# A transform and two feed-forward layers in float32r: operand tiles of 512 columns in place of 502, and padded constants

## The chip, the core and the metric

The kernel runs on one NeuronCore of a Trainium2 chip. The metric is the device time of one execution in microseconds (us). TensorE (PE in the profile) multiplies: it first loads a block of weights (PEld, 128 rows by 128 columns) and then streams a second operand, the moving one, past it, one column after the other. VectorE (DVE), ScalarE (ACT) and GpSimd (POOL) do the elementwise work, and SyncE (SP) issues most transfers. All operands of TensorE lie in SBUF, the on-chip memory of 128 partitions; an address below is a byte offset within a partition.

## The reference

`x` is 2 x 3008 x 256. Its two-dimensional Fourier transform is taken and the real part kept; the 6016 rows of 256 go through two layers of one shape, 256 to 2048 to 256, with different nonlinearities.

```python
X = np.fft.fft(np.fft.fft(x, axis=1), axis=2).real      # 2 x 3008 x 256
x = X.reshape(6016, 256)
h = x @ w_in;   x = (h * sigmoid(h)) @ w_out             # layer 1
h = x @ w_in2;  y = (h * clip(h + 3, 0, 6) / 6) @ w_out2 # layer 2
```

## The kernel before, in words

The transform (the first 50 us or so) is done with float32 matmuls against tables: `step1` (47-point, table `t1_sb`), `step2` (256-point, `t2_sb`) and `step3` (64-point, `t3_sb`), lines 350 to 413. Each float32 matmul stands as two records in the trace. The result is kept as even and odd parts in the tile `eo`, which has 3010 columns.

The layers work on six chunks of those columns, five of 502 and one of 500 (`CHUNK` and `CHUNKS`, lines 52 and 53). Precision comes from splitting each operand into a rounded high part and a remainder, both float32r (4 bytes an element), and from three matmuls for each product. That is `mm3`, lines 299 to 302, through which all the layers' matmuls go:

```python
T.matmul(o, wh, xhi, ...)   # L300: high weights, high data
T.matmul(o, wh, xlo, ...)   # L301: high weights, low data
T.matmul(o, wl, xhi, ...)   # L302: low weights, high data
```

The second argument is the weights, the third the moving operand; each of the three loads its weights anew. There are 3888 such matmuls: 3240 of 502 columns and 648 of 500.

Layer 1 runs to about 435 us of the span. `win1` and `win1_end` (551 to 573) multiply the chunk's even part, then its odd part, into `ab`; the moving operands are the halves `[:, 0]` and `[:, 1]` of the tiles `xhi` and `xlo` from `split_eo` (504). ScalarE makes `ghi`, GpSimd and VectorE make `glo` (`low`, 616), both tiles of two halves as well, and `wout1` (630) multiplies their halves into four accumulators (`y` in the rows). Layer 2 computes the hidden products by seven products instead of eight (`pa`, `pb`, `pc`, `pd`; loop from 880 on): its moving operands are the tiles `b11` to `b22` and `t1` to `t4` (`b` and `t` in the rows), made by `moving` (668), and part of its weights are sums of blocks in the tile `wx` (`load_w2`, 262). `wout2` (814) uses `ghi` and `glo` as `wout1` does.

Where these tiles begin matters to the change, so here is what the built program gives. `ghi`, `glo`, `xhi` and `xlo`, and four of the ten ring buffers of `moving` (pool `xsp`), are tiles of 2 x 502 elements, 4016 bytes a partition. Each begins 32 bytes past a multiple of 64. Its half `[:, 0]` therefore starts at 32 past, and its half `[:, 1]`, 2008 bytes later, at 56 past. The other six ring buffers (pool `xq`) are 2 x 512, and both their halves start at a multiple of 64. All the layers' weights, in `whi`, `wlo` and `wx`, start at 32 past a multiple of 64: three single-column constants `three`, `mask` and `minus` of 4 bytes, each in a slot of 32, stand ahead of them in the memory. Counted over the 3888 matmuls, the moving operand starts at

| past a multiple of 64 | which operands | matmuls | of 502 / 500 columns |
|---|---|---|---|
| 32 bytes | halves `[:, 0]` | 1704 | 1416 / 288 |
| 56 bytes | halves `[:, 1]` | 1572 | 1308 / 264 |
| 0 | both halves of the six `xq` buffers | 612 | 516 / 96 |

The order of the work is written out by hand: the loops issue each engine's instructions in the order in which they stand, and semaphores release them.

Of the kernel before, what the change touches and what calls it, by code (L numbers as in the profile page):

```python
# [36 lines left out]
F32 = mybir.dt.float32  # L37
F32R = mybir.dt.float32r
U32 = mybir.dt.uint32
I32 = mybir.dt.int32  # L40
AF = mybir.ActivationFunctionType
# [3 lines left out]
S, D, B = 3008, 256, 2  # L45
# [4 lines left out]
FF, P = 2048, 128  # L50
NF = FF // P
CHUNK = 502
CHUNKS = [(c, min(CHUNK, NPAIR - c)) for c in range(0, NPAIR, CHUNK)]


# [11 lines left out]
NEAR = 4  # L67
# [13 lines left out]
def body(tc, xh, x128, t1, t2, t3, w1, w128, w2, out):  # L81
    nc = tc.nc
    V, A, T, G = nc.vector, nc.scalar, nc.tensor, nc.gpsimd
    per = tc.alloc_tile_pool(name="per", bufs=1)
# [3 lines left out]
    eop = tc.alloc_tile_pool(name="eop", bufs=1, side="right")  # L88

    w128_sb = per.tile([P, NF], F32, name="w128_sb")  # L90
    three = per.tile([P, 1], F32, name="three")
    mask = per.tile([P, 1], F32, name="mask")
    minus = per.tile([P, 1], F32, name="minus")
    eo = eop.tile([P, 2, NPAIR], F32, name="eo", tag="eo")
    w2_d = [
        [dr.tile([P, 2, n], F32, name=f"w2{q}_d{g}", tag=f"w2{q}_d{g}") for q, n in (("h", 512), ("l", 512), ("x", 384))]
# [110 lines left out]
    wx = []  # L207
# [53 lines left out]

    def load_w2(g):
        if not wx:
            wx.append(eop.tile([P, NF // 2, 2, 384], F32R, name="wx", tag="eo"))
        weight_tiles(2, g)
        for dst, src in zip((whi[2, g], wlo[2, g], wx[0][:, g]), w2_d[g]):
            nc.sync.dma_start(dst.bitcast(F32), src)
# [37 lines left out]
    fft = tc.alloc_tile_pool(name="fft", bufs=1)  # L305
# [3 lines left out]
    nil = fft.tile([P, P], F32, name="nil")  # L309
    w128_raw = fft.tile([P, NF, 2], U32, name="w128_raw")  # L310
    t1_sb = fft.tile([P, 6 * 104], F32, name="t1_sb")
    t2_sb = fft.tile([P, 257], F32, name="t2_sb")
    sign = t2_sb[:, 256:257]
    t3_sb = fft.tile([P, P], F32, name="t3_sb")
    xl = fft.tile([P, 2, B, 2, 32], F32, name="xl")
    xr = fft.tile([P, B, 12], F32, name="xr")
    out1 = [fft.tile([P, 2, QA, 2, NJ], F32, name=f"out1_{n}") for n in range(B)]
    xt = {}
    xbuf = [xp.tile([P, k, 4 * P], F32, name=f"x{i}", tag=f"x{i}") for i, k in enumerate((1, 2, *[XB] * 4))]
# [51 lines left out]
    def step1_last():  # L371

        ps = psA.tile([P, 512], F32, name="psl", tag="s2")
        for n in range(B):
            for j in range(4):
                T.matmul(
                    ps[32 * j : 32 * j + 32, 12 * n : 12 * n + 12], xl[:, 0, n, j % 2, :],
                    t1_sb[:, 576 + 12 * j : 588 + 12 * j], start=True, stop=True,
                )
        A.activation(xr.rearrange("p n q -> p (n q)"), ps[:, 0:24], AF.Copy)  # L380


    def step2(g):
# [47 lines left out]
    A.dma_start(t1_sb[:, 0:288], t1[:, 0:288])  # L431
    for i in range(4):
        load_x(i, nc.sync, A)
    warm = fft.tile([P, 1], F32, name="warm")
    A.activation(warm, three, AF.Silu)
    V.memset(mask, 1.0)
    V.memset(mask[0:1], 0.0)
# [9 lines left out]
    i = g = 0  # L447
    busy(8)

    def step1_next():  # L450

        nonlocal folded, i
        x = folded
        if i + 1 < nx:
            folded = fold(i + 1)
        step1(i, x)
        if 3 <= i < nx - 4:
            load_x(i + 4, nc.sync, nc.sync)
        if i + 4 == nx - 1:
            load_raw(1, w1, 0)  # L460
        i += 1
        if i == 1:
            nc.sync.dma_start(t2_sb, t2)
            nc.sync.dma_start(t3_sb, t3)
            nc.sync.dma_start(xl, x128)
        if i < 3:
            busy(3 - i)
        if i == 4:
            nc.sync.dma_start(w128_raw, w128)
        if i == 5:  # L470
            G.tensor_tensor(out=xl[:, 0], in0=xl[:, 0], in1=xl[:, 1], op=ALU.add)
        if i == 7:
            step1_last()
        if i == nx - 4:
            load_raw(1, w1, 1)
            advance(steps, 1)
# [10 lines left out]
    while XCH[i][0] == 0:  # L487
        step1_next()
# [12 lines left out]
    xsp = tc.alloc_tile_pool(name="xsp", bufs=1, side="right", reuse_waits="tile")  # L501
    xs = {}

    def split_eo(k, j):
        c, n = CHUNKS[j]
        hi, lo = (xsp.tile([P, 2, CHUNK], F32R, name=f"x{h}{k}", tag=f"x{2 * (k % 2) + i}") for i, h in enumerate(("hi", "lo")))
        eb = xsp.tile([P, CHUNK], F32, name=f"eb{k}", tag="eb", bufs=2)
        new = k < len(CHUNKS)
        if new:
            nc.sync.dma_start(e128_d[j], eo[0:1, 1, c : c + n])  # L510
        nc.sync.dma_start(eb[:, :n], e128_d[j].to_broadcast([P, n]))
        if new:
            split(hi[:, :, :n], lo[:, :, :n], eo[:, :, c : c + n], x_d[j])
        else:
            for x, d in zip((hi, lo), x_d[j]):
                nc.sync.dma_start(x[:, :, :n].bitcast(F32), d)
        return hi, lo, eb
# [3 lines left out]
    units = [(k, f) for k, (_, fs) in enumerate(segs) for f in fs]  # L521
    n1 = NF * len(CHUNKS)
    turn = n1 - 10
# [4 lines left out]
    gs = {}  # L528

    def hidden_tiles():  # L530
        h = pools[0].tile([P, 2, CHUNK], F32, name="h", tag="h", bufs=2)
        ghi = pools[0].tile([P, 2, CHUNK], F32R, name="ghi", tag="ghi", bufs=4)
        return h, ghi

    def product(o, wt, x, first=True):
# [2 lines left out]
    begun, spare = {}, {}  # L538

    def even_part(k, f):  # L540

        i = units.index((k, f))
        if i < 4:
            if i % 2 == 0:
                spare[0] = pools[0].tile([P, 2, CHUNK], F32R, name=f"zg{i}", tag="glo").bitcast(F32)
            return spare[0][:, i % 2]
        if i == 4:
            spare[0] = stage_tile(1).rearrange("p m (s n) -> p (m s) n", s=2)
        return spare[0][:, i % 4]
# [25 lines left out]
    def parts(k, f):  # L575
# [6 lines left out]
    pools = [  # L582
        tc.alloc_tile_pool(name="wk", bufs=3, side="right", reuse_waits="tile"),
        tc.alloc_tile_pool(name="psH", bufs=4, space=PSUM, side="right", reuse_waits="tile"),
    ]
# [25 lines left out]
    stp = tc.alloc_tile_pool(name="stp", bufs=1, reuse_waits="tile")  # L611
    xq = tc.alloc_tile_pool(name="xq", bufs=1, reuse_waits="tile")
# [3 lines left out]
    def low(k, f, shared=False):  # L616
        n = CHUNKS[segs[k][0]][1]
        h, ghi, _ = gs[k, f]
        glo = pools[0].tile([P, 2, CHUNK], F32R, name="glo", tag="glo")
        for s, eng in ((1, G), (0, V if shared or f % 2 else G)):  # L620
            eng.tensor_tensor(out=glo[:, s, :n], in0=h[:, s, :n], in1=ghi[:, s, :n], op=ALU.subtract)  # L621
        gs[k, f] = ghi, glo
# [45 lines left out]
    def moving(k):  # L668

        j = segs2[k][0]
        n = CHUNKS[j][1]
        st = stp.tile([P, 2, 2 * CHUNK], F32, name=f"u{k}", tag="su", bufs=1)
        nc.sync.dma_start(st[:, :, : 2 * n], y1_d[j])
        b11, b12 = st[:, 0, 0:n], st[:, 0, n : 2 * n]
        b21, b22 = st[:, 1, 0:n], st[:, 1, n : 2 * n]
        us[k] = {}

        def high(name, src):  # L680
            r = ring[0] % RING
            ring[0] += 1
            x = (xsp if r < NEAR else xq).tile([P, 2, CHUNK if r < NEAR else 512], F32R, name=f"{name}_{k}", tag=f"x{r}")
            us[k][name] = x[:, 0, :n], x[:, 1, :n]
            A.activation(x[:, 0, :n], src, AF.Copy)

        def rest(name, src):
            hi, lo = us[k][name]
            (V if k == 0 and name in ("b21", "t2", "t3") else G).tensor_tensor(out=lo, in0=src, in1=hi, op=ALU.subtract)

        yield
        high("b11", b11)
        yield
        rest("b11", b11)
        high("b21", b21)
        yield
        rest("b21", b21)
        yield
        V.tensor_tensor(out=b11, in0=b12, in1=b11, op=ALU.subtract)
        V.tensor_tensor(out=b12, in0=b22, in1=b12, op=ALU.subtract)  # L700
        high("t1", b11)
        yield
        rest("t1", b11)
        yield
        V.tensor_tensor(out=b11, in0=b22, in1=b11, op=ALU.subtract)
        V.tensor_tensor(out=b21, in0=b11, in1=b21, op=ALU.subtract)
        high("t2", b11)
        yield
        rest("t2", b11)
        high("t4", b21)  # L710
        yield
        rest("t4", b21)
        high("t3", b12)
        yield
        rest("t3", b12)
        high("b22", b22)
        yield
        rest("b22", b22)
        yield
# [25 lines left out]
    for i in range(n1):  # L745
        k, f = units[i]
# [26 lines left out]
        else:  # L773
# [4 lines left out]
            q, odd = divmod(i - turn, 2)  # L778
# [25 lines left out]
        E.tensor_tensor(out=g[1][:, i, :n], in0=h[:, i, :n], in1=g[0][:, i, :n], op=ALU.subtract)  # L804

    def split_tiles():
        h = pools[0].tile([P, 2, CHUNK], F32, name="h", tag="h", bufs=2)
        ghi = pools[0].tile([P, 2, CHUNK], F32R, name="ghi", tag="ghi", bufs=4)
        glo = pools[0].tile([P, 2, CHUNK], F32R, name="glo", tag="glo")
        return h, (ghi, glo)  # L810

    y2, kept2, late = {}, {}, []
# [45 lines left out]
            nc.sync.dma_start(out[:, m, c : c + n], dst)  # L858

    def snapshot(name, n):  # L860
        t = xsp.tile([P, CHUNK], F32, name=name, tag="eb", bufs=2)
        A.activation(t[:, :n], pa[:, :n], AF.Copy)  # L862
        return t

# [8 lines left out]
    for e, (k, f) in enumerate(units2):  # L873
        j, fs = segs2[k]
        n = CHUNKS[j][1]
        u = us[k]
# [210 lines left out]
```

## Time and profile before

| | |
|---|---|
| time, median of 3 runs | 942.62 us (942.47 to 942.95) |
| time of the profiled execution | 942.65 us |
| its span, first to last instruction | 940.9 us |
| TensorE busy | 935.5 us, 99% |
| weight loads busy | 778.5 us, 83% |
| VectorE / ScalarE / GpSimd busy | 70% / 69% / 56% |
| granted TensorE clock | 1.00 of full speed |

A matmul's own duration in the trace overlaps the next one's and its end is modelled, so the 390 ns of one is not what it costs. What it costs is read from the starts: the time from one matmul's start to the next one's, called the pitch below. The starts stand in the timeline, to 0.01 us, and the count of matmuls in a long stretch gives their mean. Weight loads have rows of their own on PEld.

### The profile page before, as it was taken

Reading aid. Unit: us, or ns where it says so; the run is one execution under the profiler, and the core shown is the slowest. Engines: PE = TensorE matmul, PEld = TensorE weight load, DVE = VectorE, ACT = ScalarE, POOL = GpSimd, SP = SyncE. Lnnn points to the kernel's source line nnn. Section 1 sums busy time; section 2 is a strip of 40 time slices with the busy share of each in tenths; the row PEclk is TensorE's granted clock in tenths of the full one; section 3 lists DMA queues with packets and bytes.
Section 4 is the critical chain, followed back from the end, with each engine's and each line's share of the span. In section 5 each row is a group of like instructions: output and inputs, shape, how many; then the busy total and the mean of one; then the engine's idle time right before and its main releaser. Section 6 shows DMA issues by size and latency. Waiting matters only on the chain.

```text
span 940.9 us, 12163 instructions
## 1 busy us (share of the span) xinstructions
PE 935.5 (99%) x4286; PEld 778.5 (83%) x4286; DVE 662.8 (70%) x907; ACT 651.5 (69%) x1144; POOL 531.0 (56%) x391
## 2 busy tenths in 40 slices
PE   9999999999999999999999999999999999999998
PEld 9988888888888888888888888888888888888886
DVE  7988899979999999865554565564555555455544
ACT  4878767675767676857776777766776677677665
POOL 2056646654666656534774567655765665476543
PEclk9999999999999999999999999999999999999999
DMA  8554344052263636576130002020020002001001
GB/s 320 193 203 149 134 143 144 1 189 97 104 217 121 191 119 192 189 279 211 62 88 1 1 1 88 0 88 1 1 88 0 1 1 88 1 0 44 1 1 44
DMA packets 25160, 89.27 MB, mean 95 GB/s; under 512 B 2886, under 2 KB 11340, under 8 KB 22572
## 3 DMA queue, kind: packets, MB, share of 16 engines
q1 hardware_dynamic: 23724, 81.81, 23.9%
q0 software_dynamic: 992, 6.16, 3.4%
q8 instruction: 33, 0.54, 0.2%
q10 hardware_dynamic: 384, 0.54, 0.2%
q14 instruction: 27, 0.22, 0.1%
HBM read 52.30 MB, written 36.20 MB: 94 GB/s over the span
## 4 chain that ended last, share of the span: by engine, by line
PE 99%; DMA 0%; ACT 0%; DVE 0%; issue 0%
PE y L300 19%; PE y L302 19%; PE y L301 19%; PE ab L300 5%; PE ab L301 5%; PE ab L302 5%; PE pa L301 4%; PE pa L300 4%; PE pa L302 3%; PE pb L301 2%; PE pb L302 2%; PE pb L300 2%; PE ps L365 1%; PE ps L408 1%; PE pd L301 1%; PE pc L301 1%
## 5 line engine op out<-in xcount | busy, mean ns | idle before, releaser
L804 POOL TENSOR_TENSOR glo<-h,ghi 128x502 fp32r<-128x502 f32 (+1 forms) x191 | 247.9, 1310 | 198.7 <-ACT ghi L801 198.7
L621 POOL TENSOR_TENSOR glo<-h,ghi 128x502 fp32r<-128x502 f32 (+1 forms) x137 | 218.3, 1609 | 193.3 <-ACT h L580 180.4
L300 PE MATMUL y<-ghi,whi 128*128 128x502 f32 (+1 forms) x768 | 299.6, 390 | 0.0
L302 PE MATMUL y<-ghi,wlo 128*128 128x502 f32 (+1 forms) x768 | 299.4, 390 | 0.0
L301 PE MATMUL y<-glo,whi 128*128 128x502 f32 (+1 forms) x768 | 299.4, 390 | 0.0
L301 PEld LDWEIGHTS y<-glo,whi 128*128 128x128 f32 x768 | 145.1, 189 | 30.4
L300 PEld LDWEIGHTS y<-ghi,whi 128*128 128x128 f32 x768 | 144.8, 189 | 30.7
L302 PEld LDWEIGHTS y<-ghi,wlo 128*128 128x128 f32 x768 | 144.5, 188 | 30.1
L801 ACT ACTIVATE ghi<-h 128x502 fp32r<-128x502 f32 (+1 forms) x192 | 118.0, 624 | 46.7 <-DVE h L796 46.7
L579 ACT ACTIVATE ghi<-ab 128x502 fp32r<-128x502 f32 (+1 forms) x96 | 56.5, 588 | 89.8 <-DVE h L570 88.6
L796 DVE SCALAR_TENSOR_TENSOR h<-h,pc 128x502 f32<-128x502 f32 (+1 forms) x96 | 65.1, 678 | 72.2 <-ACT h L793 72.2
L926 DVE TENSOR_TENSOR pc<-u,pb 128x502 f32<-128x502 f32 (+1 forms) x48 | 32.9, 685 | 114.6 <-ACT u L862 114.6
L862 ACT ACTIVATE u<-pa 128x502 f32<-128x502 f32 (+1 forms) x96 | 56.8, 591 | 59.1 <-PE pa L302 58.7
L793 ACT ACTIVATE h<-pc,three 128x502 f32<-128x502 f32 (+1 forms) x96 | 64.7, 674 | 40.4 <-DVE pc L926 37.7
L559 DVE SCALAR_TENSOR_TENSOR st<-eb,w_sb,ab 128x502 f32<-128x502 f32 (+1 forms) x92 | 67.0, 728 | 17.8 <-PE ab L302 17.6
L300 PE MATMUL ab<-xhi,whi 128*128 128x502 f32 (+1 forms) x192 | 75.4, 393 | 0.0
L301 PE MATMUL ab<-xlo,whi 128*128 128x502 f32 (+1 forms) x192 | 75.1, 391 | 0.0
L302 PE MATMUL ab<-xhi,wlo 128*128 128x502 f32 (+1 forms) x192 | 75.0, 391 | 0.0
L570 DVE SCALAR_TENSOR_TENSOR h<-st,ab 128x502 f32<-128x502 f32 (+1 forms) x92 | 61.4, 667 | 7.7 <-PE ab L302 7.1
L796 DVE SCALAR_TENSOR_TENSOR h<-h,pd 128x502 f32<-128x502 f32 (+1 forms) x96 | 64.4, 671 | 1.2 <-ACT h L793 1.2
L793 ACT ACTIVATE h<-pd,three 128x502 f32<-128x502 f32 (+1 forms) x96 | 64.8, 675 | 0.6 <-DVE pd L938 0.6
L580 ACT ACTIVATE h<-h 128x502 f32<-128x502 f32 (+1 forms) x96 | 60.0, 625 | 3.0
(167 smaller groups left out, 1580.8 us busy)
## 6 DMA issues: line engine op xcount, KB each, us to landing
raw<-in_w SPq DMA_DIRECT2D x16, 1024.0 KB, 7.0
u<-y_d SPq DMA_DIRECT2D x6, 1004.0 KB, 6.9
y_d<-st SPq DMA_DIRECT2D x5, 1004.0 KB, 4.3
y_d<-st POOLq DMA_DIRECT2D x5, 1004.0 KB, 8.4
out<-st SPq DMA_DIRECT2D x20, 251.0 KB, 2.2
w2h_d<-h SPq DMA_DIRECT2D x8, 512.0 KB, 2.6
w2l_d<-t SPq DMA_DIRECT2D x8, 512.0 KB, 2.6
whi<-w2h_d SPq DMA_DIRECT2D x8, 512.0 KB, 8.6
```

Of the source, the lines that this page charges most:

```text
L300: T.matmul(o, wh, xhi, start=first, stop=False, **group)
L301: T.matmul(o, wh, xlo, start=False, stop=False, **group)
L302: T.matmul(o, wl, xhi, start=False, stop=last, **group)
L559: V.scalar_tensor_tensor(out=z[:, :n], in0=eb[:, :n], scalar=w128_sb[:, f : f + 1], in1=ab[:, :n], op0=ALU.mult, op1=ALU.add)
L570: V.scalar_tensor_tensor(out=h[:, 0, :n], in0=z[:, :n], scalar=2.0, in1=ab[:, :n], op0=ALU.mult, op1=ALU.subtract)
L580: A.activation(h[:, s, :n], src, AF.Silu)
L621: eng.tensor_tensor(out=glo[:, s, :n], in0=h[:, s, :n], in1=ghi[:, s, :n], op=ALU.subtract)
L793: A.activation(h[:, i, :n], c[:, :n], AF.Relu, bias=three)
L796: V.scalar_tensor_tensor(out=h[:, i, :n], in0=h[:, i, :n], scalar=6.0, in1=c[:, :n], op0=ALU.min, op1=ALU.mult)
L801: A.activation(g[0][:, i, :n], h[:, i, :n], AF.Copy)
L804: E.tensor_tensor(out=g[1][:, i, :n], in0=h[:, i, :n], in1=g[0][:, i, :n], op=ALU.subtract)
L862: A.activation(t[:, :n], pa[:, :n], AF.Copy)
```

## The change

Every tile of 2 x 502 or 502 elements that holds a moving operand, or that shares memory with one, becomes 2 x 512 or 512 wide (`LINE = 512`); the same 502 or 500 columns are used. The constants `three`, `mask`, `minus` and `warm` become columns of one tile of 16 elements (64 bytes). `t2_sb`, `xr`, `wx` and the staging tile `u` are padded, so that what stands behind them starts at a multiple of 64 bytes.

In the built program all 3888 moving operands and all 3888 weight blocks of the layers start at a multiple of 64. Counted from a multiple of 128, the moving operands start at 64, the blocks in `whi` and `wlo` at 0, and those in `wx` at 64. In the transform most operands become aligned too.

No instruction is added, removed or moved: each of the five engines has the same rows in the same order. Three things differ in form. The copies of `xhi` and `xlo` run over 2 x 502 elements in place of 1004 that lie in one piece, on ScalarE and VectorE and in the transfers. The copy to `xr` writes 2 x 12 in place of 24. And around the start of layer 1, where the tiles take over the transform's memory, one copy of `xhi` and one transfer to `eb` no longer wait for what used that memory before, and a wait for two transfers passes from one copy of `ghi` to the next but one.

```diff
 CHUNK = 502
+LINE = 512
...
-    three = per.tile([P, 1], F32, name="three")
-    mask = per.tile([P, 1], F32, name="mask")
-    minus = per.tile([P, 1], F32, name="minus")
+    consts = per.tile([P, 16], F32, name="consts")
+    three, mask, minus, warm = (consts[:, i : i + 1] for i in range(4))
...
-            wx.append(eop.tile([P, NF // 2, 2, 384], F32R, name="wx", tag="eo"))
+            flat = eop.tile([P, NF * 384 + 8], F32R, name="wx", tag="eo")[:, : NF * 384]
+            wx.append(flat.rearrange("p (g i c) -> p g i c", i=2, c=384))
...
-    t2_sb = fft.tile([P, 257], F32, name="t2_sb")
+    t2_sb = fft.tile([P, 272], F32, name="t2_sb")
...
-    xr = fft.tile([P, B, 12], F32, name="xr")
+    xr = fft.tile([P, B, 16], F32, name="xr")
...
     def split_eo(k, j):
-        hi, lo = (xsp.tile([P, 2, CHUNK], F32R, name=f"x{h}{k}", tag=f"x{2 * (k % 2) + i}") for i, h in enumerate(("hi", "lo")))
-        eb = xsp.tile([P, CHUNK], F32, name=f"eb{k}", tag="eb", bufs=2)
+        hi, lo = (xsp.tile([P, 2, LINE], F32R, name=f"x{h}{k}", tag=f"x{2 * (k % 2) + i}") for i, h in enumerate(("hi", "lo")))
+        eb = xsp.tile([P, LINE], F32, name=f"eb{k}", tag="eb", bufs=2)
...
     def hidden_tiles():
-        h = pools[0].tile([P, 2, CHUNK], F32, name="h", tag="h", bufs=2)
-        ghi = pools[0].tile([P, 2, CHUNK], F32R, name="ghi", tag="ghi", bufs=4)
+        h = pools[0].tile([P, 2, LINE], F32, name="h", tag="h", bufs=2)
+        ghi = pools[0].tile([P, 2, LINE], F32R, name="ghi", tag="ghi", bufs=4)
...
-        glo = pools[0].tile([P, 2, CHUNK], F32R, name="glo", tag="glo")
+        glo = pools[0].tile([P, 2, LINE], F32R, name="glo", tag="glo")
...
     def moving(k):
-        st = stp.tile([P, 2, 2 * CHUNK], F32, name=f"u{k}", tag="su", bufs=1)
+        st = stp.tile([P, 4 * CHUNK + 8], F32, name=f"u{k}", tag="su", bufs=1)
+        st = st[:, : 4 * CHUNK].rearrange("p (m c) -> p m c", m=2)
...
-            x = (xsp if r < NEAR else xq).tile([P, 2, CHUNK if r < NEAR else 512], F32R, name=f"{name}_{k}", tag=f"x{r}")
+            x = (xsp if r < NEAR else xq).tile([P, 2, LINE], F32R, name=f"{name}_{k}", tag=f"x{r}")
```

The same replacement of `CHUNK` by `LINE` is made in `even_part`, `split_tiles` and `snapshot`.

## Rows read from the trace of the kernel before

**Rows 1.** The page: engines' busy time, granted clock, the chain that ended last.
```profile
PE 935.5 (99%) x4286; PEld 778.5 (83%) x4286; DVE 662.8 (70%) x907; ACT 651.5 (69%) x1144; POOL 531.0 (56%) x391
...
PEclk9999999999999999999999999999999999999999
...
PE 99%; DMA 0%; ACT 0%; DVE 0%; issue 0%
```

**Rows 2.** Waits of PE: who was waited for, us in total, times, longest.
```profile
PE psw L348 <- POOL nil L426: 1.0, 1, 1.0
PE ps L362 <- ACT out L367: 0.3, 1, 0.3
```

**Rows 3.** Windows, layers: busy us and instruction count by engine, clock, DMA share, GB/s.
```profile
60.00:936.00 876.00, 876.00 (x3837) 722.78 (x3837) 610.76 (x821) 609.10 (x1050) 516.12 (x376) 1.00 0.25 84
```

**Rows 4.** Timeline of PE, transform's end: start, us, engine, line, operation, operands.
```profile
43.95 0.47 PE L300 MATMUL ab<-xhi,whi 128*128 128x502 f32 x1
44.26 0.39 PE L301 MATMUL ab<-xlo,whi 128*128 128x502 f32 x1
...
46.42 0.47 PE L300 MATMUL ab<-xhi,whi 128*128 128x502 f32 x1
```

**Rows 5.** Timeline of PE, the aligned class's first, and the layers' last rows.
```profile
435.05 0.39 PE L300 MATMUL pa<-b,whi 128*128 128x502 f32 x1
...
923.69 0.39 PE L302 MATMUL pa<-t,wx 128*128 128x500 f32 x1
...
933.93 0.39 PE L302 MATMUL y<-ghi,wlo 128*128 128x500 f32 x1
...
936.41 0.39 PE L301 MATMUL y<-glo,whi 128*128 128x500 f32 x1
936.64 0.39 PE L302 MATMUL y<-ghi,wlo 128*128 128x500 f32 x1
```

**Rows 6.** Timeline of PEld in the transform; the last number counts the loads merged.
```profile
21.15 1.87 PEld L365 LDWEIGHTS ps<-t_sb,x 128*128 128x128 f32 x16
...
23.83 0.97 PEld L408 LDWEIGHTS ps<-t_sb,o 128*128 128x128 f32 x8
```

**Rows 7.** Timeline of PE in layer 2, products with `wx`.
```profile
604.31 0.39 PE L301 MATMUL pb<-t,wx 128*128 128x502 f32 x1
604.53 0.42 PE L302 MATMUL pb<-t,wx 128*128 128x502 f32 x1
604.78 0.41 PE L300 MATMUL pa<-t,wx 128*128 128x502 f32 x1
605.03 0.42 PE L301 MATMUL pa<-t,wx 128*128 128x502 f32 x1
605.28 0.40 PE L302 MATMUL pa<-t,wx 128*128 128x502 f32 x1
605.52 0.39 PE L300 MATMUL y<-ghi,whi 128*128 128x502 f32 x1
```

**Rows 8.** Timeline of PEld, the loads beside the first of these matmuls.
```profile
604.31 0.19 PEld L302 LDWEIGHTS pb<-t,wx 128*128 128x128 f32 x1
604.54 0.19 PEld L300 LDWEIGHTS pa<-t,wx 128*128 128x128 f32 x1
```

**Rows 9.** The transfers of `xhi` and `xlo`: count, KB each, median us to landing.
```profile
xh_d<-xhi SPq DMA_DIRECT2D x5, 502.0 KB, 4.6
...
xlo<-xl_d SPq DMA_DIRECT2D x5, 502.0 KB, 10.6
```

More of the change, by code (lines that the diff above doesn't have):

```diff
@@ L379, in step1_last @@
                 )
-        A.activation(xr.rearrange("p n q -> p (n q)"), ps[:, 0:24], AF.Copy)
+        A.activation(xr[:, :, 0:12], ps[:, 0:24].rearrange("p (n q) -> p n q", n=B), AF.Copy)
     def step2(g):
@@ L433, in body @@
         load_x(i, nc.sync, A)
-    warm = fft.tile([P, 1], F32, name="warm")
     A.activation(warm, three, AF.Silu)
@@ L462, in step1_next @@
         if i == 1:
-            nc.sync.dma_start(t2_sb, t2)
+            nc.sync.dma_start(t2_sb[:, 0:257], t2)
             nc.sync.dma_start(t3_sb, t3)
@@ L544, in even_part @@
             if i % 2 == 0:
-                spare[0] = pools[0].tile([P, 2, CHUNK], F32R, name=f"zg{i}", tag="glo").bitcast(F32)
+                spare[0] = pools[0].tile([P, 2, LINE], F32R, name=f"zg{i}", tag="glo").bitcast(F32)
             return spare[0][:, i % 2]
@@ L806, in split_tiles @@
     def split_tiles():
-        h = pools[0].tile([P, 2, CHUNK], F32, name="h", tag="h", bufs=2)
-        ghi = pools[0].tile([P, 2, CHUNK], F32R, name="ghi", tag="ghi", bufs=4)
-        glo = pools[0].tile([P, 2, CHUNK], F32R, name="glo", tag="glo")
+        h = pools[0].tile([P, 2, LINE], F32, name="h", tag="h", bufs=2)
+        ghi = pools[0].tile([P, 2, LINE], F32R, name="ghi", tag="ghi", bufs=4)
+        glo = pools[0].tile([P, 2, LINE], F32R, name="glo", tag="glo")
         return h, (ghi, glo)
@@ L860, in snapshot @@
     def snapshot(name, n):
-        t = xsp.tile([P, CHUNK], F32, name=name, tag="eb", bufs=2)
+        t = xsp.tile([P, LINE], F32, name=name, tag="eb", bufs=2)
         A.activation(t[:, :n], pa[:, :n], AF.Copy)
```

## Prediction

> **What bounds the kernel now.** I read the page first, then the waits of TensorE, then the timeline of TensorE and of its weight loads. On the page [rows 1] TensorE is busy for 935.5 of 940.9 us at a granted clock of 1.00, and the chain that ended last is 99% TensorE. In the list of its waits [rows 2] all of the span comes to 1.3 us. So no other engine and no transfer sets the time, and the only question is what one matmul costs.
>
> That isn't its duration but the pitch, from one start to the next. Between 60 and 936 us there are 3837 matmuls [rows 3], so 876 / 3837 = 228.3 ns each. The clock of 1.00 is the 2.4 GHz level, at which 502 columns, one a cycle, take 209.2 ns. Every matmul of the layers thus pays some 19 ns beyond its columns. I call that the excess; over all 3888 it is about 75 us, and only there can the place of operands matter.
>
> To see whether it matters I took the pitches from the timeline, subtracted the columns at 2.4 GHz, and averaged by where the moving operand starts past a multiple of 64 bytes. Ten pitches above 270 ns, around waits, and the last matmul are left out.
>
> - 32 past: 1699 pitches, the first starting at 43.95 us [rows 4], the last at 936.41 [rows 5]; excess 18.3 ns.
> - 56 past: 1568 pitches, from 46.42 [rows 4] to 933.93 [rows 5]; excess 19.7 ns.
> - 0 past: 610 pitches, from 435.05 to 923.69 [rows 5]; excess 20.8 ns. With weights in `whi` and `wlo` it is 18.9 (334 pitches), with `wx` 23.1 (276).
>
> The uncertainty of each of these means is 0.1 to 0.4 ns. The mean of all is 19.3 ns.
>
> So the aligned operands that the kernel already has are the dearest class, not the cheapest. But all weights stand at 32 past. What the cheapest class shares is that data and weights have the same place within 64 bytes.
>
> **The change part by part.**
>
> *Moving operands and weights.* The weights of the next matmul load while the present one streams: the loads start together with the matmuls, 604.31 and 604.31, 604.54 and 604.53 [rows 7, 8]. Two streams are read from the same memory at once, so I take the excess to depend on the place of one against the other. After the change the difference is 0 within 64 bytes for all pairs, as it is now for the 32-past class. Then the other two classes come down to 18.3 ns:
>
> - 1572 x (19.7 - 18.3) = 2.2 us,
> - 612 x (20.8 - 18.3) = 1.5 us,
>
> 3.7 us in all. No row shows weights at 0 past with a stream of 502 columns, so both ends have to be bounded. Downwards: the whole excess goes, 3888 x 19.3 = 75 us. Upwards: all pairs behave as the aligned data with `wx` do, 3888 x (23.1 - 19.3) = 15 us more. I take 3.7, from the nearest rows, those with the same difference.
>
> *The dear pairs.* In rows 7 the pitches from 604.53 on are 0.25, 0.25, 0.25 and 0.24 us. Of the 610 aligned pitches 54 are 240 to 250 ns, always with `wx`, and most come in such runs. Against 228 they cost 54 x 18 = 1.0 us, part of the 1.5 above. Most aligned pairs with `wx` run without it, so this is a state that a run of equal matmuls falls into. Data at 0 and weights at 32 past are gone after the change, but all pairs are then equal, which is the ground of a rival below.
>
> *The transform.* Its pitch is that of the weight loads: with `x` as weights (32 past), (1.87 - 0.19) / 15 = 112.0 ns; with `o` as weights and `t3_sb` as data, both already at a multiple of 64, (0.97 - 0.19) / 7 = 111.4 ns [rows 6]. These agree within the 0.01 us of the rows. I take 0 for some 400 records; a half nanosecond each would be 0.2 us.
>
> *Copies and transfers in other shapes.* The six copies each of `xhi` and `xlo` over 2 x 502 and the changed waits lie on engines that TensorE waits for by 1.3 us in the whole run [rows 2]; that is also the most that shifted waits can give back. The 24 transfers of `xhi` and `xlo` have rows of 2008 bytes where 4016 lay together. They land after 4.6 to 10.6 us [rows 9]. A loaded chunk is asked for at least five units ahead of its first use, and a unit is 18 matmuls, 4.1 us, so there are some 20 us of cover. If the landing doubled to 21.2 us, the six loads would come some 1 us late each, 6 us at most. I take 0, since the bytes are the same.
>
> *Elementwise work at aligned addresses.* GpSimd is busy 516 of 876 us and VectorE 611 [rows 3]. If they became a tenth slower or faster, TensorE would see it only through the waits of rows 2, so 0; the time from the last matmul at 936.64 us [rows 5] to the end of the span is a few copies and a transfer, and no term changes it.
>
> **Sum.** The profiled execution took 942.65 us, 0.03 above the median of 942.62, with 1.75 us outside its span. 942.65 - 3.7 = 938.9 us, 0.4% less.
>
> **A rule weighed.** The pitch of rows 3 is 228.3 ns. By the Trainium skill, "TensorE: Matmul & The Clock Gate", section "Back-to-back issue gap", an isolated warm matmul costs its columns at 2.4 GHz and 2.5 ns, measured on bf16; that is 211.7 ns here. The trace disagrees by 16.6 ns. If float32r at bad places were the whole cause, aligning would give 65 us, an estimate from that page. The third rival carries its chance, by the rows alone.
>
> **The rivals.**
>
> 1. *The place doesn't matter, only what runs beside it.* The means by class differ also in role: the 32-past ones are the first halves, the 0-past ones belong to layer 2 only. Then the aligned class keeps its present costs and all matmuls join it: 3456 with `whi` and `wlo` at 18.9 and 432 with `wx` at 23.1, together 75.3 us against 75.0 now. The time would be 943.0. For it: with `whi` the aligned class is within 0.6 ns of the best. Against it: halves 32 and 56 past alternate within the same unit, on the same engines' work, and still differ by 1.4 ns, many times the uncertainty.
>
> 2. *Slower: equal pairs lock into the dear state.* Now three kinds of places alternate, which breaks a run of equal matmuls after three to six. After the change every pair has the same places within 64 bytes, nothing breaks the run, and pitches of 0.25 us as in rows 7 become common. It decides from about 280 locked pitches more than now: at 18 to 20 ns each they outweigh the 3.7 us and 1.9 us beyond. If all went as the aligned class does on average, it is 3888 x (20.8 - 19.3) = 5.8 us more, 948.5; if as that with `wx`, 957.4. For it: the state occurs only where both data halves are aligned. Against it: it occurs only with data and weights 32 bytes apart, never in the 32-past class.
>
> 3. *A large gain.* If the excess is the price of weights at 32 past, it goes as a whole or in good part: 867 us at the most, 905 for half. For it: the excess is paid by all 3888 matmuls, and misplaced weights are the one thing that all share. Against it: the transform's loads have the same pitch with weights at 0 and at 32 past [rows 6], and data at 0 past gain nothing.
>
> 4. *Only the 56-past operands gain.* They alone start in the middle of 16 bytes; 0 and 32 are multiples. Then 1572 x 1.4 = 2.2 us goes and the rest stays: 940.4. The 0-past class at 20.8 against 18.3 speaks against it, its part with `whi` at 18.9 for it. This is the granularity that the Trainium skill gives in "SBUF — State Buffer", specifications: lines of 16 bytes. By that rule padding from 32 to 64 buys nothing; the trace neither confirms nor refutes it.
>
> **How the numbers follow.** Within 0.2%, about 1.9 us, a measurement of this kernel can't tell a difference from none. Chances: the forecast 0.35, with its own range 936 to 941; rival 1 0.25; rival 2 0.20; rival 3 0.10; rival 4 0.10. Faster: nearly all of the forecast (0.31), all of rival 3, more than half of rival 4 (0.06), 0.47. Within 0.2%: the rest of these and most of rival 1, 0.28. Slower: rival 2 and the upper edge of rival 1 with late transfers, 0.25. For 8 in 10 the range leaves out most of rival 3 and the dear end of rival 2: 930 to 953 us.
>
> **What would show it.** Right: the count of matmuls from 60 to 936 us rises from 3837 by some 15, the pitch goes to 227.4 ns, no pitches of 240 to 250 ns with `wx` remain, both halves of `ghi` have the same pitch, and the transform's load pitch stays at 111 to 112 ns. Rival 2 shows as pitches of 0.24 to 0.25 us in `y` or `ab` rows; rival 3 as a pitch under 222 ns everywhere; rival 1 as halves that still differ. I am wrong in a further way if TensorE's waits grow past 1.3 us: then a transfer or an engine came in late, and the row of the waits names it.

## The result, and the profile after

The changed kernel takes 934.09 us (median of 5 runs, 934.04 to 934.83) against 942.62: a ratio of 0.9911, 95% interval 0.9896 to 0.9925. It is 8.5 us faster, where 3.7 had been forecast. Line numbers of the kernel after are one higher in most places: the three matmuls of `mm3` are L301 to L303.

The page of the kernel after, engines' busy time, clock and the chain, against [rows 1]:

```profile
PE 926.3 (99%) x4286; PEld 775.2 (83%) x4286; DVE 659.5 (71%) x907; ACT 651.8 (70%) x1144; POOL 530.8 (57%) x391
...
PEclk9999999999999999999999999999999999999999
...
PE 98%; DMA 0%; DVE 0%; issue 0%; ACT 0%; SPq 0%; DVEq 0%
```

TensorE still sets the time alone, at the same clock. Its waits after, against [rows 2]:

```profile
PE psw L349 <- POOL nil L427: 1.0, 1, 1.0
PE ps L366 <- DVE x L341: 0.4, 2, 0.3
PE ps L363 <- ACT out L368: 0.3, 1, 0.3
```

They sum to 1.7 us against 1.3, so nothing was won by less waiting. The time came from the pitch. A window in which all of the layers' matmuls have 502 columns shows it, first before, then after (busy us and count by engine; the count, x1662 and x1676, includes the matmuls that reach into the window):

```profile
450.00:830.00 380.00, 380.00 (x1662) 313.05 (x1661) 209.44 (x325) 268.56 (x458) 236.32 (x186) 1.00 0.10 32
```

```profile
450.00:830.00 380.00, 380.00 (x1676) 314.49 (x1676) 212.65 (x329) 270.22 (x459) 238.29 (x188) 1.00 0.09 28
```

That is 14 matmuls more in 380 us, 228.6 and 226.7 ns each. Over all pitches up to 270 ns, taken from the starts as in the prediction, 502 columns went on average from 228.6 to 226.7 ns and 500 columns from 227.0 to 222.2. So 3240 x 1.88 = 6.1 us and 648 x 4.84 = 3.1 us; longer gaps around a few waits (14 pitches above 270 ns in place of 10) take 0.5 us back. That leaves 8.7, against the span's 940.9 - 932.3 = 8.6.

The means hide the plainest sign. These are six of the last matmuls of the kernel after, 500 columns each, against the last two of [rows 5]:

```profile
924.91 0.38 PE L302 MATMUL y<-glo,whi 128*128 128x500 f32 x1
925.13 0.38 PE L303 MATMUL y<-ghi,wlo 128*128 128x500 f32 x1
925.35 0.38 PE L301 MATMUL y<-ghi,whi 128*128 128x500 f32 x1
925.57 0.38 PE L302 MATMUL y<-glo,whi 128*128 128x500 f32 x1
925.79 0.38 PE L303 MATMUL y<-ghi,wlo 128*128 128x500 f32 x1
926.01 0.38 PE L301 MATMUL y<-ghi,whi 128*128 128x500 f32 x1
```

Every pitch is 0.22 us, and they stay so to the end. Before, the last eleven pitches, all of first halves, ran 226, 228, 221, 226, 224, 229, 222, 225, 229, 226, 225 ns. The pitch did not only get smaller, it became steady: 75% of the 500-column pitches with `whi` and `wlo` are at 220 ns after, 2% before.

The products with `wx`, the counterpart of [rows 7]:

```profile
598.87 0.39 PE L301 MATMUL pb<-t,wx 128*128 128x502 f32 x1
599.10 0.39 PE L302 MATMUL pb<-t,wx 128*128 128x502 f32 x1
599.33 0.39 PE L303 MATMUL pb<-t,wx 128*128 128x502 f32 x1
599.55 0.39 PE L301 MATMUL pa<-t,wx 128*128 128x502 f32 x1
```

The runs of 0.25 us are gone: pitches of 240 to 270 ns number 4 after and 64 before. And the halves of `ghi`, at 502 columns, now cost the same: 226.7 and 226.7 ns, where the first had cost 227.2 and the second 229.1. The transform's loads are as in [rows 6], (1.87 - 0.19) / 15 = 112.0 and (0.97 - 0.19) / 7 = 111.4 ns:

```profile
20.98 1.87 PEld L366 LDWEIGHTS ps<-t_sb,x 128*128 128x128 f32 x16
...
23.66 0.97 PEld L409 LDWEIGHTS ps<-t_sb,o 128*128 128x128 f32 x8
```

And the transfers of [rows 9] land half a microsecond later, hidden as before:

```profile
xh_d<-xhi SPq DMA_DIRECT2D x5, 502.0 KB, 5.1
...
xlo<-xl_d SPq DMA_DIRECT2D x5, 502.0 KB, 11.0
```

### The profile page after: what moved, and what is told of

The parts are those of the page before. It is cut to its first block, busy times and chain, and to the rows that moved or that the text cites. A ratio compares the mean times of both kernels' runs of the same rounds, so it can differ in the third digit from the quotient of the medians.

```text
span 932.3 us, 12162 instructions
## 1 busy us (share of the span) xinstructions
PE 926.3 (99%) x4286; PEld 775.2 (83%) x4286; DVE 659.5 (71%) x907; ACT 651.8 (70%) x1144; POOL 530.8 (57%) x391
## 4 chain that ended last, share of the span: by engine, by line
PE 98%; DMA 0%; DVE 0%; issue 0%; ACT 0%; SPq 0%; DVEq 0%
PE y L301 19%; PE y L302 18%; PE y L303 18%; PE ab L301 5%; PE ab L302 5%; PE ab L303 5%; PE pa L301 4%; PE pa L302 4%; PE pa L303 3%; PE pb L302 2%; PE pb L301 2%; PE pb L303 2%; PE ps L366 1%; PE ps L409 1%; PE pd L302 1%; PE pd L301 1%
## 5 line engine op out<-in xcount | busy, mean ns | idle before, releaser
L301 PE MATMUL y<-ghi,whi 128*128 128x502 f32 (+1 forms) x768 | 298.0, 388 | 0.0
L303 PE MATMUL y<-ghi,wlo 128*128 128x502 f32 (+1 forms) x768 | 297.8, 388 | 0.0
L303 PEld LDWEIGHTS y<-ghi,wlo 128*128 128x128 f32 x768 | 144.2, 188 | 29.3
L301 PEld LDWEIGHTS y<-ghi,whi 128*128 128x128 f32 x768 | 144.2, 188 | 29.0
L794 ACT ACTIVATE h<-pc,consts 128x502 f32<-128x502 f32 (+1 forms) x96 | 64.6, 673 | 40.1 <-DVE pc L927 39.0
L301 PE MATMUL ab<-xhi,whi 128*128 128x502 f32 (+1 forms) x192 | 75.2, 392 | 0.1
L303 PE MATMUL ab<-xhi,wlo 128*128 128x502 f32 (+1 forms) x192 | 74.5, 388 | 0.0
L794 ACT ACTIVATE h<-pd,consts 128x502 f32<-128x502 f32 (+1 forms) x96 | 64.7, 674 | 0.6 <-DVE pd L939 0.6
```

Of the source, the lines that this page charges most:

```text
L301: T.matmul(o, wh, xhi, start=first, stop=False, **group)
L303: T.matmul(o, wl, xhi, start=False, stop=last, **group)
L794: A.activation(h[:, i, :n], c[:, :n], AF.Relu, bias=three)
```

## The experiments

All are timed beside the kernel before, which took 942.8 to 943.0 us in these runs. "Distance" below is the start of the moving operand less the start of the weights, in bytes; "relation" is that distance within 64 bytes, so relation 0 is a pair with the same place in its 64. Means leave out pitches above 270 ns, and "excess" is again what a pitch has beyond its columns at 2.4 GHz.

**Weights aligned, data as before.** From the kernel before, only the constants and `u` are padded:

```diff
-    three = per.tile([P, 1], F32, name="three")
-    mask = per.tile([P, 1], F32, name="mask")
-    minus = per.tile([P, 1], F32, name="minus")
+    consts = per.tile([P, 16], F32, name="consts")
+    three, mask, minus, warm = (consts[:, i : i + 1] for i in range(4))
...
-        st = stp.tile([P, 2, 2 * CHUNK], F32, name=f"u{k}", tag="su", bufs=1)
+        st = stp.tile([P, 4 * CHUNK + 8], F32, name=f"u{k}", tag="su", bufs=1)
```

> The kernel before with only the weights in whi and wlo moved to a multiple of 64 bytes (constants in one padded tile, u padded); wx and all moving operands stay. Theory R, the relation of data and weights within 64 bytes decides: only the 336 pairs of aligned data with whi and wlo come to the excess of 16.9 ns of the changed kernel; data at 32 past stand 32 off now and go to 18.9 ns or more, data at 56 stay near 19.7; 942 to 943 us. Rival W, the weights' own place decides: all 3456 with whi and wlo come to 16.9, 3456 x 2.4 = 8 us less, about 934.5. Rival D, the data's own place: nothing changes, 942.6.

Measured: 943.35 us, ratio 1.0010 (1.0001 to 1.0020). The weights' own place is worth nothing; rival 3's ground is gone. But the 336 pairs that now were both at a multiple of 64 had an excess of 18.8 ns, not 16.9. Theory R, which had the time about right, missed there.

**Data aligned, weights as before.** From the changed kernel, the weights go back to 32 past, by the three constants in tiles of their own, `u` without its padding, and

```diff
-            flat = eop.tile([P, NF * 384 + 8], F32R, name="wx", tag="eo")[:, : NF * 384]
+            flat = eop.tile([P, NF * 384 + 8], F32R, name="wx", tag="eo")[:, 8 : 8 + NF * 384]
```

> The changed kernel with all weights back at 32 past a multiple of 64 (three constants in tiles of their own, u unpadded, wx begun 32 bytes later), all 3888 moving operands at a multiple of 64. Theory R: every pair is 32 off, excess 18.9 with whi and wlo and 23.1 with wx as in the kernel before, 943 us. Rival D, the data's own place: 934. Rival E, equal places of all pairs let them settle into one rhythm, whatever the places are: below 939, with pitches of 502 columns heaped on one value.

Measured: 941.86 us, ratio 0.9989 (0.9980 to 0.9999); excess 18.9 ns with `whi` and `wlo`, as theory R had it, and 19.4 for the 502 columns among them. Aligned data by themselves give next to nothing, and equal pairs alone (theory E) don't either. Yet the pitches of 502 columns heap on a few values, 224, 229, 230 and 231 ns: steady, but at a dear value.

**Everything 32 past.** From the changed kernel, constants as before and `wx` without padding (that of `u` stays, other than the expectation says; in the built program all operands of the layers are 32 past all the same):

```diff
-            flat = eop.tile([P, NF * 384 + 8], F32R, name="wx", tag="eo")[:, : NF * 384]
-            wx.append(flat.rearrange("p (g i c) -> p g i c", i=2, c=384))
+            wx.append(eop.tile([P, NF // 2, 2, 384], F32R, name="wx", tag="eo"))
```

> The changed kernel with every weight and every moving operand 32 bytes past a multiple of 64 (wx and u unpadded, three constants in tiles of their own). Theory R: relation 0 as in the changed kernel, 934 us, 226.7 ns for most pitches of 502 columns and 220 for those of 500. Rival A, both must lie at a multiple of 64 as such: like the 32-past class before, excess 18.3, 939 us, and no heap at 220 for 500 columns.

Measured: 934.13 us, ratio 0.9908 (0.9893 to 0.9923), the excess 16.9 ns, the heaps at 227 and 220. No operand of the layers lies at a multiple of 64, and the whole gain is there. In the layers' operands this kernel differs from the one with only the data aligned by the data's 32 bytes alone:

```profile
450.00:830.00 380.00, 380.00 (x1662) 313.33 (x1661) 209.50 (x324) 268.32 (x458) 235.44 (x186) 1.00 0.10 32
```

```profile
450.00:830.00 380.00, 380.00 (x1677) 314.43 (x1676) 212.38 (x328) 270.28 (x460) 238.88 (x188) 1.00 0.09 29
```

The first is the window with aligned data and weights 32 past (x1662), the second that with both 32 past (x1677). What counts is data against weights.

**Padding alone.** The changed kernel with `LINE = CHUNK` and the tiles of `moving` as before:

```diff
-LINE = 512
+LINE = CHUNK
...
-            x = (xsp if r < NEAR else xq).tile([P, 2, LINE], F32R, name=f"{name}_{k}", tag=f"x{r}")
+            x = (xsp if r < NEAR else xq).tile([P, 2, CHUNK if r < NEAR else 512], F32R, name=f"{name}_{k}", tag=f"x{r}")
```

> The changed kernel with its padding alone: the tiles are 2 x 502 again, so second halves start 24 bytes past a multiple of 64, while weights, first halves and the six wide buffers start at a multiple of 64. 2316 pairs have relation 0, 1572 stand 24 off. Theory P, each pair has its own price whatever runs around it, 16.9 ns for relation 0 as in the changed kernel and 19.7 for 24 off: mean 18.0 against 19.3, 4.9 us less, 938. Theory C, the low price comes only where all pairs around are alike: relation 0 costs 18.3 in mixed company as the 32-past class before, mean 18.9, 941 us.

Measured: 942.13 us, ratio 0.9990 (0.9980 to 0.9999). The 1925 pairs of 502 columns at relation 0 keep an excess of 18.5 ns: theory P falls. Theory C's 18.3 ns and 941 us are within 1.2 us.

**Wide tiles alone.** The changed kernel with constants, `wx` and `u` as before (only `u` is shown; the padding of the transform's `t2_sb` and `xr` stays):

```diff
-        st = stp.tile([P, 4 * CHUNK + 8], F32, name=f"u{k}", tag="su", bufs=1)
-        st = st[:, : 4 * CHUNK].rearrange("p (m c) -> p m c", m=2)
+        st = stp.tile([P, 2, 2 * CHUNK], F32, name=f"u{k}", tag="su", bufs=1)
```

> The changed kernel with its wide tiles alone, nothing padded: weights at 32 past a multiple of 64, 3276 moving operands at 32 past (relation 0), the 612 of the six ring buffers at 0 past, as before. Layer 1 then has relation 0 throughout, layer 2 is mixed. Theory P: 3276 at 16.9, the aligned 612 at their old 20.8, mean 17.5, 6.9 us less, about 936. Theory C: layer 1 and 500-column stretches without the odd buffers reach the price of the changed kernel, layer 2 stays near 18.3 to 19 where the odd buffers stand among the others, about 938 to 939.

Measured: 934.82 us, ratio 0.9911 (0.9897 to 0.9925). Layer 1 has the price of the changed kernel (16.7 ns in both), but layer 2 is no dearer for relation 0 (16.5), with the odd buffers among them at 19.4. So it isn't that any unlike neighbour spoils a pair, as theory C said; the time is 3.2 us below its 938, and 1.2 below theory P's 936.

Side by side, the same window of the padded kernel (x1666) and of the wide one (x1675):

```profile
450.00:830.00 380.00, 380.00 (x1666) 313.69 (x1665) 210.21 (x326) 269.02 (x458) 237.06 (x186) 1.00 0.10 32
```

```profile
450.00:830.00 380.00, 380.00 (x1675) 314.36 (x1674) 212.14 (x328) 269.60 (x458) 238.56 (x188) 1.00 0.09 29
```

What sets these two apart stands in the built programs. Tiles of 2 x 502 lie 4032 bytes apart, which is 64 less than a multiple of 256, so the distance changes from tile to tile. Tiles of 2 x 512 lie 4096 apart, so it doesn't. Counted within 256 bytes, the distance differs from that of the matmul before in 2857 of 3883 cases in the kernel before, 2825 in the padded one, 345 in the wide and in the changed one. That gave theory K, and a test that keeps every operand at a multiple of 64.

**Multiples of 64, changing distance.** The changed kernel with halves of 528 elements; `u` takes a buffer of the raw weights, since the wider tiles need the room.

```diff
-LINE = 512
+LINE = 528
...
-        st = stp.tile([P, 4 * CHUNK + 8], F32, name=f"u{k}", tag="su", bufs=1)
+        st = dp.tile([P, 4 * 512], F32, name=f"u{k}", tag="raw")
```

> The changed kernel with halves 528 elements wide in place of 512 (the staging tile u takes a buffer of the raw weights to make room). All moving operands and weights still start at multiples of 64 bytes, as the change asks, but halves lie 2112 bytes and tiles 4224 bytes apart, so the distance between data and weights takes eight values within 512 bytes where the changed kernel has one for 80% of its matmuls. Theory 64, places within 64 bytes decide: 934. Theory K, the pitch settles only if the distance between data and weights stays the same from matmul to matmul, within 128 bytes or more: excess 18.5 as in the padded kernel without wide tiles, about 941.

Measured: 939.03 us, ratio 0.9958 (0.9944 to 0.9972), excess 18.2 ns, no heaps. Its window:

```profile
450.00:830.00 380.00, 380.00 (x1671) 314.35 (x1670) 211.31 (x327) 270.51 (x460) 237.59 (x188) 1.00 0.10 31
```

Alignment as the change words it gives 3.9 us, not 8.5; theory K's 941 was 2 us too much. The rest, 4.6 to 4.9 us, needs a distance that stays the same, and not any: it stays at 160 for 80% of the matmuls in the kernel with aligned data and weights 32 past, which took 941.9 us. A rival here is that each distance has its own price, and that this kernel merely holds fewer pairs at the cheap 192. Its trace speaks against that: its 500-column pairs at 192 within 256 average 226.1 ns (180 pitches), those of the changed kernel 221.1 (527).

**Which distance.** Six chunks of 500 columns (the last 10 columns are left out), and in layer 1 each chunk's data begin a different number of elements into their tiles. Each scan was executed once, and only its pitches are read.

```diff
+SHIFT = (0, 4, 12, 16, 48, 80)
+
+
+def shifted(pool, j, **names):
+    t = pool.tile([P, 2 * LINE + 128], F32R, **names)
+    return t[:, SHIFT[j] : SHIFT[j] + 2 * LINE].rearrange("p (i c) -> p i c", i=2)
```

> The changed kernel with six chunks of 500 columns (the last 10 columns are left out), in layer 1 with the data of chunks 1 to 6 at distances of 192, 208, 240, 256, 384 and 0 bytes from the weights, within 512; layer 2 stays at 192. Only the pitches of layer 1 are read, some 288 for each distance. Theory K with a period of 64: 192, 256, 384 and 0 all settle at 220.0; 208 and 240 stand off and cost 224 or more. With a period of 128: 192 at 220.0, 256, 384 and 0 alike among themselves but at another value. With 512 or more: all differ. Theory 64: 192, 256, 384 and 0 are equal, as the first.

The second scan, with `SHIFT = (96, 64, 32, 112, 124, 120)`:

> As the scan before it, six chunks of 500 columns with the last 10 columns left out, now with the layer 1 data at distances of 64, 448, 320, 128, 176 and 160 bytes from the weights, within 512. In that scan 192 settled at 220.0 and 0, 256, 384 and 208 at 226.7. A period of 128 bytes: 64, 320 and 448 all settle at 220.0 as 192. A period of 256: 448 at 220.0, the others at 226.7. A period of 512 or more: none of them is bound to be 220.0. 160 should lie near 223.8, the value of 500 columns in the kernel with all weights put back by 32 bytes, whose pairs stand there.

Measured, mean pitch of layer 1 at 500 columns (278 to 288 pitches each):

| distance within 512 | ns | distance + 256 | ns |
|---|---|---|---|
| 192 | 220.7 | 448 | 220.5 |
| 0 | 226.7 | 256 | 226.6 |
| 128 | 226.8 | 384 | 226.7 |
| 64 | 228.8 | 320 | 228.6 |
| 160, 176 | 223.8, 226.5 | | |
| 208, 240 | 226.8, 224.8 | | |

Stretches of 22 us in which one distance alone runs show the same in their counts. In this order the distances are 192, 0 and 256 (first scan), then 448, 64 and 320 (second scan):

```profile
193.00:215.00 22.00, 22.00 (x102) 18.77 (x101) 17.12 (x22) 15.22 (x28) 11.62 (x10) 1.00 0.57 202
152.00:174.00 22.00, 22.00 (x99) 18.26 (x98) 21.97 (x26) 14.79 (x25) 13.23 (x8) 1.00 0.45 152
348.00:370.00 22.00, 22.00 (x99) 18.25 (x98) 21.71 (x28) 15.16 (x28) 13.98 (x9) 1.00 0.72 192
```

```profile
252.00:274.00 22.00, 22.00 (x102) 18.78 (x101) 21.90 (x27) 15.93 (x28) 12.95 (x10) 1.00 0.83 243
193.00:215.00 22.00, 22.00 (x98) 18.22 (x97) 16.67 (x21) 14.63 (x27) 11.51 (x9) 1.00 0.60 202
300.00:322.00 22.00, 22.00 (x98) 18.21 (x97) 21.60 (x24) 13.62 (x24) 15.12 (x10) 1.00 0.76 215
```

The pairs 256 apart agree within 0.2 ns: a period of 256 bytes, the second of the alternatives. Its clause that the others lie at 226.7 missed for 64 and 320. The value for 160 came out as expected. The first scan's idea that multiples of 64 are equal is refuted; the changed kernel's 192 happens, with 448, to be the best of the twelve.

**Which width.** The changed kernel with chunks of different widths, executed once (the last 36 columns are left out):

```diff
-CHUNK = 502
+CHUNK = 504
+WIDTHS = (504,500,498,496,492,484)
...
-CHUNKS = [(c, min(CHUNK, NPAIR - c)) for c in range(0, NPAIR, CHUNK)]
+CHUNKS = [(sum(WIDTHS[:i]), n) for i, n in enumerate(WIDTHS)]
```

> The changed kernel with chunks of 504, 500, 498, 496, 492 and 484 columns; the last 36 columns of the work are left out. Only the pitch per width is read. Theory Q, in aligned state the pitch moves in steps of 6.67 ns, 16 columns at 2.4 GHz, as 226.7 for 502 and 220.0 for 500 suggest: 504 at 226.7, 500 at 220.0, 498 and 496 at 220.0, 492 at 220.0 or 213.3, 484 at 213.3. Rival, no steps: about 0.42 ns a column, 504 at 227.5, 496 near 224, 484 near 219, and the 220.0 of 500 columns belongs to the last chunk's surroundings, not to its width.

The second, executed once, has `WIDTHS = (512,510,508,506,488,486)`, `CHUNK = 512` and `u` in a buffer of the raw weights:

> The changed kernel with chunks of 512, 510, 508, 506, 488 and 486 columns; the staging tile u takes a buffer of the raw weights so that the wider tiles fit. Only the pitch per width is read. If the pitch moves in steps of 6.67 ns and columns alone decide the step, 506 to 512 lie at 226.7 or 233.3 and 486 and 488 at 220.0. If a constant excess of 17 to 19 ns holds, 512 costs 231, 506 costs 228, 488 costs 221. Widths of 484 to 504 have shown both: heaps at 220.0 and 226.7, but 496 and 498 dearer than 500.

Measured, mean pitch with `whi` and `wlo`:

| columns | 484 | 486 | 488 | 492 | 496 | 498 | 500 | 504 | 506 | 508 | 510 | 512 |
|---|---|---|---|---|---|---|---|---|---|---|---|---|
| ns | 219.4 | 220.2 | 220.3 | 220.7 | 224.6 | 226.4 | 222.1 | 228.9 | 230.2 | 228.7 | 227.5 | 232.9 |

Neither theory holds. There are heaps near 220 and 227, but 500 columns cost less than 496 and 510 less than 506. That 500 is cheap as a width, and not as the last chunk, is shown: here it is the second chunk. Nine in ten of these pitches are at a distance of 192 within 256; what another distance would make of a width isn't shown.

**Chunks of 500.** Same work, `WIDTHS = (500, 500, 500, 500, 500, 510)`, with `u` as in the kernel of 528.

> The changed kernel with five chunks of 500 columns and one of 510 in place of five of 502 and one of 500, same work; the staging tile u takes a buffer of the raw weights to make room. Theory S, a width of 500 has its pitch of 222.2 ns by its own: 3240 x 222.2 + 648 x about 231 = 869.6 us for the layers against 3240 x 226.7 + 648 x 222.2 = 878.5, so about 925. Rival, the price of 500 belonged to the last chunk, or a pitch of 510 columns near 238 and a late staging tile eat it up: 930 to 936.

Measured: 926.77 us, ratio 0.9826 (0.9812 to 0.9840). Theory S, with about 925, holds; 510 came at 227 rather than 231.

**One distance for all.** The same chunks, and `wx` and the six ring buffers moved to the distance of the rest, 192:

```diff
-            flat = eop.tile([P, NF * 384 + 8], F32R, name="wx", tag="eo")[:, : NF * 384]
+            flat = eop.tile([P, NF * 384 + 136], F32R, name="wx", tag="eo")[:, 80 : 80 + NF * 384]
...
-        return stp.tile([P, 2, 2 * CHUNK], F32, name=f"st{i}", tag=f"st{i}")
+        t = stp.tile([P, 4 * CHUNK + 24], F32, name=f"st{i}", tag=f"st{i}")
+        return t[:, : 4 * CHUNK].rearrange("p (m c) -> p m c", m=2)
```

> Five chunks of 500 columns and one of 510, and wx and the six ring buffers moved so that all 3888 pairs stand 192 bytes apart within 512; in the kernel with these chunks before it, wx and the ring buffers stood at 0 and 320. Theory K: the disturbed pitches around wx and the ring buffers go, 3240 at 220.3 and 648 at 226.8, 860.8 us for the layers against 865 in that kernel, 922 to 923 us. Theory 64: no difference to that kernel, 926.8.

Measured: 922.55 us, ratio 0.9784 (0.9771 to 0.9798), faster than both kernels. In its window and its timeline, layer 2 with products of all kinds:

```profile
450.00:830.00 380.00, 379.97 (x1725) 322.79 (x1724) 218.89 (x340) 276.33 (x474) 246.51 (x193) 1.00 0.09 27
```

```profile
600.25 0.38 PE L304 MATMUL pb<-b,wx 128*128 128x500 f32 x1
600.48 0.38 PE L302 MATMUL pa<-b,whi 128*128 128x500 f32 x1
600.70 0.38 PE L303 MATMUL pa<-b,whi 128*128 128x500 f32 x1
600.91 0.38 PE L304 MATMUL pa<-b,wlo 128*128 128x500 f32 x1
601.13 0.38 PE L302 MATMUL pc<-b,whi 128*128 128x500 f32 x1
```

97% of its 500-column pitches with `whi` and `wlo` are at 220 ns and 99% of those with `wx`; the distance never changes. Its waits of TensorE have grown, to 5.0 us from the 1.7 of the changed kernel, most of it in this row:

```profile
PE ab L302 <- DVE st L560: 3.0, 4, 1.3
```

## Why the prediction was right or wrong

- *What bounds the kernel.* Right. The pitch moved; the clock and the transform's loads stayed. The waits, whose growth past 1.3 us was named as a sign of a further mistake, came to 1.7, with 0.4 for VectorE's folding of the transform's `x` and none for a transfer; that is small against 8.5.
- *The mechanism of the forecast, data against weights.* Right that it's the relation: the kernel all 32 past and the one with only the data aligned show it. That 64 bytes are its scale was wrong: 0, 64, 128 and 192 are equal within 64, and in the scans they cost 226.7, 228.8, 226.8 and 220.7 ns. The kernel of 528, where only the places within 64 are equalized, has about the gain that was worked out, 3.9 us for 3.7 and an excess of 18.2 for 18.3. But its distances also take four values within 256 bytes where the kernel before has ten, and no run separates the two.
- *"Then the other two classes come down to 18.3 ns."* This is the step that was mis-sized. All classes came to 16.9 or below, because the 32-past class was not itself at its best: its distance took many values within 256 bytes, and the wide tiles made it one for 80% of the matmuls. The rows of before could not show that price, but the sizes of the tiles, 4032 and 4096 bytes apart, were there to be seen, and the means by class were taken within 64 bytes only.
- *500 columns.* The forecast gave the 500-column matmuls nothing of their own; they fell by 4.8 ns, 3.1 us of the 8.5.
- *The number.* Right in direction and inside 930 to 953, but outside the forecast's own 936 to 941: 934.1. The 4.6 to 4.9 us beyond the kernel of 528 are luck in so far as nothing in the forecast chose the distance. The change happens to put it at 192; at a constant 160 next to nothing is won.
- *The dear pairs.* They went, as said. They were a matter of distance and not of aligned data: in the kernel with aligned data and weights 32 past, 43 pitches of 240 to 270 ns were left. Nor do they belong to `wx`, as the forecast read them. All 54 stand at a distance of 96 within 256, and when the weights alone were aligned, pairs with `whi` and `wlo` came to 96 too, and at 502 columns averaged 230.3 ns; 22 pitches of such pairs are 240 to 270 ns.
- *Rival 2, equal pairs lock.* Half right. Equal pairs do settle into a rhythm, but which one depends on the distance. At 160 bytes it gave 941.9 us, at 192 it gave 934.1. That it would be the dear one was the wrong half.
- *Rival 1* (the place doesn't matter), *rival 3* (misplaced weights) and *rival 4* (16 bytes) are refuted in this order by the kernel all 32 past beside the one with only the data aligned, by the weights alone, and by 192 against 208 and 128 in the scan. With rival 4 goes the reading of the Trainium skill's 16-byte lines ("SBUF — State Buffer", specifications) as the only granularity here.
- *Transform, copies, transfers, elementwise work at 0.* Right; the transfers' 0.4 to 0.5 us stayed hidden.
- *The Trainium skill's 2.5 ns beyond the columns* for an isolated matmul ("TensorE: Matmul & The Clock Gate", "Back-to-back issue gap") isn't reached by any kernel here: the best excess, 500 columns at 220 ns, is 11.7 ns.

What stays open is why. The runs show a dependence on the distance with a period of 256 bytes and on its constancy; which part of the memory or of TensorE makes it wasn't measured. Nor was a distance off a multiple of 16 bytes held constant, or one between 64 and 128: 24 and 96 occur only among others. And in each kernel here the weights in `whi` and `wlo` start at one place within 256 bytes, so the distance changed only where the data's start did; data and weights that move together from matmul to matmul weren't tried.

## What to carry to other kernels

Where TensorE is busy throughout and its pitch exceeds its columns, look at where the moving operand lies against the weights, and at whether that distance stays the same from matmul to matmul: tiles at a stride that is a multiple of 256 bytes keep it. Which constant distance is cheap has to be measured: 192 won 8.5 us here, 160 only 1.0. All of this is shown for float32r in this one kernel. Alignment by itself is a poor name for it; padding for alignment alone gave 0.8 us here and the wide tiles alone 8.1. And try the width: 500 columns were cheaper than 502 by more than their two columns.

## What the hardware showed unexpectedly

- The pitch depends on the distance between data and weights with a period of 256 bytes: 220.7 and 220.5 ns at 192 and 448, 228.8 and 228.6 at 64 and 320, for 500 columns. The dearest mean at 502 columns is that of 96, 232.9 ns in the kernel before (228 pitches).
- It isn't monotone in columns: 226.4 ns for 498, 222.1 for 500, 226.8 for 502, 230.2 for 506, 227.5 for 510.
- The sequence of pitches repeats. The last eleven of the padded kernel are 227, 228, 220, 226, 224, 230, 222, 224, 229, 227, 224 ns, those of the kernel before within 1 ns of it one by one, with these operands 32 bytes elsewhere but at the same distances. Over the layers, 99% of the pitches of the kernel all 32 past are within 1 ns of their counterparts in the changed kernel; between the kernels before and after it is 28%. Most of what looks like noise of 3 ns follows the addresses.
